# Attention's TensorE work grouped by two units, and one rounding of k moved from ScalarE to GpSimd

## The chip, the cores and the metric

The kernel runs on one core of a Trainium2 chip. The metric is the device time of one execution in microseconds (us). The engines are called as the profile calls them: PE (TensorE, matmuls), PEld (its weight loads), DVE (VectorE), ACT (ScalarE), POOL (GpSimd) and SP (SyncE, which issues most DMAs). Each engine works through its own queue of instructions in a fixed order.

## The reference

Causal attention over 2 batches, 12 heads, 448 positions and a head size of 64 is followed by two feed-forward blocks of width 768 with 3072 hidden units; ahead of the second stands a Fourier mixing. Everything is asked for in 32-bit floats.

```python
scores = q @ k.T / 8 ; scores above the diagonal = -1e9
attn = softmax(scores) ; x = attn @ v                  # heads side by side: x is [2, 448, 768]
x = x + relu(layernorm(x) * g @ w_ch1) @ w_ch2          # first feed-forward
u = x + real(fft(fft(x, over positions), over features))
out = u + relu(layernorm(u) @ w_ch1') @ w_ch2'          # second feed-forward
```

## The kernel before

**Precision.** A product that must be exact to more than one rounded operand is done as three matmuls: each operand is split into a rounded part ("hi", type fp32r) and what is left ("lo"), and hi x lo, lo x hi and hi x hi are added up in PSUM. q is split in `split_q` (POOL for all but the first two pairs), k in `split_k`: the rounded part (scaled by -1/8) is made at L251 by DVE for the first pair and at L253 by ACT for the other eleven; the rest is made by DVE at L254, which reads the rounded part.

**Attention.** The 24 heads are taken as 12 pairs of heads, and each pair as four units (`UNITS`). Units 0 and 1 are query blocks 0 and 2 of either head, unit 2 is query block 1 of both, unit 3 the last 64 queries of both. There are 48 units in all. A unit goes through these steps, each a small function:

- `scores` (PE, L282): the matmuls into PSUM tiles `sps`. Units 0 and 1 are done in one call. The matmuls of units 0 to 2 use 64 rows of the array (the two heads lie in its two halves), those of unit 3 all 128.
- `row_max` (DVE, L299) and `exps` (ACT, L311): mask and row maximum, then exponential and row sum into the SBUF tile `pexp`.
- `transposes` (PE, L355): four 128x128 transposes into a PSUM tile `tps`; `transposed` (ACT, L360) copies it to SBUF as `pT`.
- `values` (PE, L374): the product with v, added up in `avps`. The matmuls use 64 columns of the array for either head. Unit 0 is done with unit 1.

Once a pair: `sum_recip` (DVE, L320 to L323) makes reciprocals of the row sums; `spread` (PE, L330) transposes them and ACT copies them out (`divrow`, L334); `spread_rows` (PE, L340 and L344) spreads them over the partitions and ACT copies the result out (`inv`, L349); `scaled` (DVE, L399) multiplies. For half of the pairs `moved` (POOL, L410 and L411) issues two DMAs that shift the rows by one partition.

**The order.** One loop with step i, one step a unit, writes the whole attention down. In step i of the kernel before, PE gets the transposes of unit i-1, the scores of unit i+3 and the values of unit i-3; DVE gets the row maximum of unit i; ACT gets the copy of unit i-1's transposes and then the exponentials of unit i. Between them lie the splits of q and k for later pairs (`splits`: for pair p at steps 4(p-2) and 4(p-2)+1, the first pairs by `SPLIT_AT`), the loads of the raw q, k and v, and from step 32 on the first loads and conversions of feed-forward weights (`w_load`, `w_tick`: two ACT and four DVE instructions on 128x768 for each weight tile, L167 to L174, L91 and L92). `sum_recip`, `spread` and `spread_rows` come one, two and three steps after the first of the next pair begins. The layer norm of batch 0 (`ln_rest`) is put into the later steps by `bg_step`.

The framework takes this text as priorities: a planner places instructions in each engine's queue by its own estimate of when they can start, so that work of later steps can come ahead of work that it holds to be late. After that the queues are fixed. PSUM tiles `sps`, `tps` and the one of `spread` come from a pool of seven banks, and `avps` has the eighth. A tile takes a bank when the last reader of an earlier one is done.

After attention the feed-forward of batch 0 starts (`ff_lead`, matmuls `hps`), then the rest; nothing there is touched by the change.

Of the kernel before, what the change touches and what calls it, by code (L numbers as in the profile page):

```python
# [14 lines left out]
ACTF = mybir.ActivationFunctionType  # L15
# [4 lines left out]
B, H, S, D = 2, 12, 448, 64  # L20
# [4 lines left out]
PAIRS = [3, 4, 5, 0, 1, 2]  # L25
# [5 lines left out]
ES = 4  # L31
W_LOAD, W_FROM, W_EARLY = 32, 38, 6
SPLIT_AT = {1: (1, 1), 2: (2, 5)}
AHEAD, L_T, L_C, L_V = (3, 1, 2, 3)
Q_AT, K_AT = (0, 1)
NB1, NB2 = 3, 6
NJ = DM // P
HJ = NJ // 2
# [14 lines left out]
def fused_kernel(ctx: ExitStack, tc: tile.TileContext, aps, out):  # L53
    nc = tc.nc
# [147 lines left out]
    q_raw, v_raw, qparts, zparts, kparts = {}, {}, {}, {}, {}  # L202
# [44 lines left out]
    def split_k(b, pr):  # L247
        k = kparts[b, pr] = t_tile([P, 2, S], "ks")
        src = q_raw[b, pr][:, 1]
        if (b, pr) == pairs[0]:  # L250
            yield nc.vector.tensor_scalar_mul(k[:, 0], src, -(D**-0.5))  # L251
        else:
            yield nc.scalar.activation(out=k[:, 0], in_=src, func=ACTF.Copy, scale=-(D**-0.5))  # L253
        yield nc.vector.scalar_tensor_tensor(  # L254
            out=k[:, 1], in0=src, scalar=-(D**-0.5), in1=f32(k[:, 0]), op0=ALU.mult, op1=ALU.subtract
        )
# [5 lines left out]
    def scores(i):  # L262

        b, pr, unit = units[i]
        if i in s_ps:
            return
        q, k, z = qparts[b, pr], kparts[b, pr], zparts[b, pr]
        now = [i, i + 1] if unit == UNITS[0] else [i]
        banks = {}
        for u in now:  # L270
            s_ps[u] = {n: bank("sps") for n in sorted({seg[2] for seg in units[u][2]})}
        work = sorted([(seg[1], u, seg) for u in now for seg in units[u][2]], key=lambda w: w[0])
        for blk in dict.fromkeys(w[0] for w in work):
            segs = [w for w in work if w[0] == blk]
            for qu, ku in ((0, 0), (1, 0), (0, 1)):
                for _, u, (r, blk, at, c, _) in segs:
                    n = min(P * (blk + 1), S)
                    if r is None:
                        lhsT, rhs = z[:, qu], k[:, ku, :n]
                    else:  # L280
                        lhsT, rhs = q[own[r], qu, blk * P : (blk + 1) * P], k[own[r], ku, :n]
                    nc.tensor.matmul(  # L282
                        out=s_ps[u][at][:, c : c + n], lhsT=lhsT, rhs=rhs, start=(qu + ku == 0), stop=(ku == 1),
                        skip_group_check=True,
                    )
# [19 lines left out]
    def exps(i):  # L305
        b, pr, unit = units[i]
        e = exp_tiles[i % ES]
        flat = e.rearrange("p a b -> p (a b)")
        sp, st = s_ps.pop(i), stat[b, pr]
        for col, at, c, to, n in widths(unit):  # L310
            nc.scalar.activation(  # L311
                out=flat[:, to : to + n], in_=sp[at][:, c : c + n], func=ACTF.Exp, scale=-1.0, bias=st[:, 0, col : col + 1],
                accum_out=st[:, 1, col : col + 1],
            )
        p_sb[i] = e

    def sum_recip(b, pr):

        st, d = stat.pop((b, pr)), psm.tile([P, 2, NT], F32R, tag="dv", name="div")
        nc.vector.tensor_scalar_add(st[:, 1], st[:, 1], 1e-9)  # L320
        nc.vector.reciprocal(out=st[:, 2], in_=st[:, 1])
        nc.vector.tensor_copy(out=d[:, 0], in_=st[:, 2])
        nc.vector.tensor_tensor(out=d[:, 1], in0=st[:, 2], in1=f32(d[:, 0]), op=ALU.subtract)  # L323
        diag[b, pr] = d
# [26 lines left out]
    def transposes(i):  # L351
        e = p_sb.pop(i)
        tp = bank("tps")
        for a in range(4):
            nc.tensor.transpose(out=tp[:, a * P : (a + 1) * P], in_=e[:, a], identity=ident)  # L355
        t_ps[i] = tp

    def transposed(i):
        t = t_tile([P, 4, P], "pT", F32)
        nc.scalar.activation(  # L360
            out=t.rearrange("p a q -> p (a q)"), in_=t_ps.pop(i), func=ACTF.Copy
        )
        pT[i] = t

    def values(i):
        b, pr, unit = units[i]
        if unit == UNITS[0]:
            return
        if unit == UNITS[1]:
            av[b, pr] = one_bank("avps")  # L370
        o, vv = av[b, pr], v_raw[b, pr]

        def add(r, cols, key, blocks, p):
            nc.tensor.matmul(  # L374
                out=o[own[r], cols], lhsT=vv[:, r, key], rhs=p, start=(key == 0), stop=(key == blocks - 1),
                skip_group_check=True,
            )

        if unit == UNITS[1]:
            p = pT.pop(i - 1), pT.pop(i)  # L380
            for blk, c in ((0, 0), (2, 1)):
                for key in range(blk + 1):
                    for r in range(2):
                        add(r, slice(blk * P, (blk + 1) * P), key, blk + 1, p[r][:, c + key])
        elif unit == UNITS[2]:
            p = pT.pop(i)
            for key in range(2):
                for r in range(2):
                    add(r, slice(P, 2 * P), key, 2, p[:, 2 * r + key])
        else:  # L390
            p = pT.pop(i)
            for key in range(4):
                for r in range(2):
                    add(r, slice(3 * P, S), key, 4, p[:, key, own[r]])
            del v_raw[b, pr]

    def scaled(b, pr):
        xt = px.tile([P, S], F32, tag="x", name="x") if pr < HJ else p_tile("xr")
        nc.vector.tensor_tensor(out=xt, in0=av.pop((b, pr))[:, :S], in1=inv.pop((b, pr)), op=ALU.mult)  # L399
        xa[b, pr] = xt  # L400
        if pr < HJ:
            x[b, pr] = xt

    def moved(b, pr):

        for j in range(HJ, NJ):
            if (b, j) not in x:
                x[b, j] = px.tile([P, S], F32, tag="x", name="x")
        xt = xa[b, pr]
        nc.gpsimd.dma_start(out=x[b, pr][1:], in_=xt[: P - 1])  # L410
        nc.gpsimd.dma_start(out=x[b, HJ + (pr + 1) % HJ][:1], in_=xt[P - 1 :])  # L411
# [4 lines left out]
    def ln_sum(b, j, src=x):  # L416
        if b not in ln_acc:
            ln_acc[b], n_acc[b] = src[b, j], 1
            return
        acc = ln_acc[b]  # L420
        if n_acc[b] == 1:
            ln_acc[b] = p_tile("lnacc")
        n_acc[b] += 1
        nc.vector.tensor_tensor(out=ln_acc[b], in0=acc, in1=src[b, j], op=ALU.add)
# [270 lines left out]
    def ln_first():  # L695
        now, *after = ln_rest(0, g_sb)
        bg.extend(now)
        late.append(after)

    later = {}  # L700
    i = 0
    while i < n + L_V or max(later, default=0) >= i:
        pi, at = divmod(i, per)
        if 0 <= i - L_T < n:
            transposes(i - L_T)
        while scored <= min(i + AHEAD, n - 1) and units[scored][:2] in kparts:
            scores(scored)
            scored += 1
        if i < n:
            red = row_max(i)  # L710
        if 0 <= i - L_C < n:
            transposed(i - L_C)
        for f in later.pop(i, []):
            f()
        if i == 0:
            exps(0)
        for f, p in splits.pop(i, []):
            for _ in f(*pairs[p]) or ():
                pass
        if at == 2 and pi + 3 < len(pairs):  # L720
            load_pair(*pairs[pi + 3])
        if i >= W_LOAD and n_raw[0] < n_split[0] + 2:
            w_load()
        if i >= W_FROM:
            w_tick(1, W_EARLY)
        with tc.issue_after(red.ins):
            bg_step()
        if 0 < i < n:
            exps(i)
        if 0 <= i - L_V < n:  # L730
            values(i - L_V)
            b, pr, _ = units[i - L_V]
            if (i - L_V) % per == per - 1:
                scaled(b, pr)
                ln_sum(b, pr, xa)
                if pr >= HJ:
                    later.setdefault(i + 1, []).append(lambda b=b, pr=pr: moved(b, pr))
                if (b, pr) == (0, PAIRS[-1]):
                    later.setdefault(i + 1, []).append(lambda: ln_first())
        if i < n and i % per == per - 1:  # L740
            b, pr, _ = units[i]
            later.setdefault(i + 1, []).append(lambda b=b, pr=pr: sum_recip(b, pr))
            later.setdefault(i + 2, []).append(lambda b=b, pr=pr: spread(b, pr))
            later.setdefault(i + 3, []).append(lambda b=b, pr=pr: spread_rows(b, pr))
        i += 1
    raw_ahead[0] = 2
    while bg:
# [145 lines left out]
```

## Time and profile before

| | us |
|---|---|
| median of 3 runs | 860.5 (857.07 to 861.02) |
| the profiled execution | 857.58 |
| its span, first to last instruction | 855.7 |
| attention's first matmul | 4.89 |
| first feed-forward matmul | 107.13 |

| engine | busy us | share of the span |
|---|---|---|
| PE | 841.3 | 98% |
| PEld | 756.6 | 88% |
| DVE | 599.1 | 70% |
| ACT | 331.9 | 39% |
| POOL | 46.0 | 5% |

In a timeline a line gives the start of a group of like instructions in us, how long they took together, the engine, the line of the code, the operation, what it writes and reads, its shape and the count; in brackets stands how long the engine had been idle before and on what. The shape before a matmul's output is rows*columns of the array that it uses. The end of a matmul is modelled, so a matmul's row overlaps the next one's; the distance from start to start is what counts.

### The profile page before, as it was taken

Reading aid. Unit: us, or ns where it says so; the run is one execution under the profiler, and the core shown is the slowest. Engines: PE = TensorE matmul, PEld = TensorE weight load, DVE = VectorE, ACT = ScalarE, POOL = GpSimd, SP = SyncE. Lnnn points to the kernel's source line nnn. Section 1 sums busy time; section 2 is a strip of 40 time slices with the busy share of each in tenths; the row PEclk is TensorE's granted clock in tenths of the full one; section 3 lists DMA queues with packets and bytes.
Section 4 is the critical chain, followed back from the end, with each engine's and each line's share of the span. In section 5 each row is a group of like instructions: output and inputs, shape, how many; then the busy total and the mean of one; then the engine's idle time right before and its main releaser. Section 6 shows DMA issues by size and latency. Waiting matters only on the chain.

```text
span 855.7 us, 11863 instructions
## 1 busy us (share of the span) xinstructions
PE 841.3 (98%) x4664; PEld 756.6 (88%) x4664; DVE 599.1 (70%) x1019; ACT 331.9 (39%) x627; POOL 46.0 (5%) x91
## 2 busy tenths in 40 slices
PE   6999999999999999999999999999999999999997
PEld 5776789899999999999998889899999999999997
DVE  5789999796666566666699789696666566666432
ACT  6898975323332333223234245322332233223200
POOL 5433000100000000000101000000000000000000
PEclk9999999999999999999999999999999999999999
DMA  5434644333333333333615203324333332320011
GB/s 205 136 103 133 201 151 171 117 105 117 111 111 110 111 111 111 111 111 107 204 60 197 74 1 105 117 74 149 110 101 109 102 100 107 111 74 1 1 65 64
DMA packets 21431, 93.28 MB, mean 109 GB/s; under 512 B 2768, under 2 KB 4568, under 8 KB 21376
## 3 DMA queue, kind: packets, MB, share of 16 engines
q1 hardware_dynamic: 19152, 86.68, 29.9%
q0 software_dynamic: 2080, 5.62, 2.1%
q8 instruction: 36, 0.59, 0.3%
q10 hardware_dynamic: 144, 0.23, 0.1%
q14 instruction: 19, 0.16, 0.1%
HBM read 88.40 MB, written 2.75 MB: 107 GB/s over the span
## 4 chain that ended last, share of the span: by engine, by line
PE 93%; DVE 3%; ACT 2%; DMA 1%; issue 1%; DVEq 0%; ACTq 0%; SPq 0%
PE hps L97 14%; PE hps L96 14%; PE hps L95 14%; PE yps L95 14%; PE yps L97 14%; PE yps L96 14%; PE sps L282 2%; PE tps L355 2%; PE avps L374 2%; ACT pexp L311 1%; DVE sps L299 1%; PE mixps L95 1%; PE mixps L96 1%; PE mixps L97 1%; PE abps L95 1%
## 5 line engine op out<-in xcount | busy, mean ns | idle before, releaser
L95 PE MATMUL yps<-h,wsp 128*128 128x448 f32 x576 | 211.3, 367 | 0.0
L97 PE MATMUL hps<-xn,wsp 128*128 128x448 f32 x576 | 211.0, 366 | 0.0
L95 PE MATMUL hps<-xn,wsp 128*128 128x448 f32 x576 | 211.0, 366 | 0.0
L96 PE MATMUL yps<-h,wsp 128*128 128x448 f32 x576 | 210.7, 366 | 0.0
L96 PE MATMUL hps<-xn,wsp 128*128 128x448 f32 x576 | 210.6, 366 | 0.0
L97 PE MATMUL yps<-h,wsp 128*128 128x448 f32 x576 | 210.5, 365 | 0.0
L91 ACT ACTIVATE wsp<-wbits 128x768 fp32r<-128x768 f32 x96 | 80.9, 842 | 171.1 <-PE yps L97 159.2
L167 ACT ACTIVATE wbits<-wraw 128x768 f32<-128x768 f32 x96 | 86.3, 899 | 95.2 <-DVE wsp L92 94.5
L95 PEld LDWEIGHTS hps<-xn,wsp 128*128 128x128 f32 x576 | 108.2, 188 | 9.2 <-issue 0.4
L96 PEld LDWEIGHTS yps<-h,wsp 128*128 128x128 f32 x576 | 108.2, 188 | 9.1 <-issue 0.6
L97 PEld LDWEIGHTS hps<-xn,wsp 128*128 128x128 f32 x576 | 108.2, 188 | 9.1 <-issue 0.2
L96 PEld LDWEIGHTS hps<-xn,wsp 128*128 128x128 f32 x576 | 108.2, 188 | 9.0 <-issue 0.2
L95 PEld LDWEIGHTS yps<-h,wsp 128*128 128x128 f32 x576 | 108.2, 188 | 8.9 <-issue 0.4
L97 PEld LDWEIGHTS yps<-h,wsp 128*128 128x128 f32 x576 | 108.2, 188 | 8.8 <-issue 0.2
L517 ACT ACTIVATE h<-hps 128x448 fp32r<-128x448 f32 x96 | 52.2, 545 | 147.9 <-PE hps L97 147.7
L518 DVE SCALAR_TENSOR_TENSOR h<-hps,h 128x448 fp32r<-128x448 f32 x96 | 59.4, 621 | 69.3 <-ACT h L517 69.2
L539 DVE TENSOR_TENSOR x<-x,yps 128x448 f32<-128x448 f32 x96 | 58.9, 617 | 68.3 <-PE yps L97 68.2
L92 DVE TENSOR_TENSOR wsp<-wbits,wsp 128x768 fp32r<-128x768 f32 x96 | 91.9, 957 | 19.0 <-ACT wsp L91 14.2
L168 DVE TENSOR_SCALAR wbits<-wbits 128x768 uint32<-128x768 uint32 x96 | 53.5, 557 | 64.0 <-ACT wbits L167 63.4
L170 DVE SCALAR_TENSOR_TENSOR wbits<-wraw,wbits 128x768 uint32<-128x768 uint32 x96 | 91.8, 956 | 2.3
L174 DVE SCALAR_TENSOR_TENSOR wbits<-wraw,wbits 128x768 uint32<-128x768 uint32 x96 | 92.0, 959 | 0.4
L311 ACT ACTIVATE pexp<-sps,stat 128x128 f32<-128x128 f32 (+3 forms) x84 | 41.3, 506 | 8.3 <-DVE stat L299 7.6
(123 smaller groups left out, 644.8 us busy)
## 6 DMA issues: line engine op xcount, KB each, us to landing
wraw<-in_w SPq DMA_DIRECT2D x96, 768.0 KB, 4.2
qkv<-in_qk SPq DMA_DIRECT2D x11, 448.0 KB, 4.8
qkv<-in_v SPq DMA_DIRECT2D x12, 256.0 KB, 5.3
out_t<-x SPq DMA_DIRECT2D x12, 224.0 KB, 1.9
x<-xr POOLq DMA_DIRECT2D x6, 222.2 KB, 4.0
cd<-in_cd POOLq DMA_DIRECT2D x3, 386.0 KB, 4.0
sd<-in_sd POOLq DMA_DIRECT2D x3, 386.0 KB, 6.2
cs<-in_cs POOLq DMA_DIRECT2D x2, 448.0 KB, 5.0
```

The lines of the kernel that those rows point to most:

```text
L91: nc.scalar.activation(out=hi, in_=src, func=ACTF.Copy)
L92: nc.vector.tensor_tensor(out=lo, in0=src, in1=f32(hi), op=ALU.subtract)
L95: nc.tensor.matmul(out=dst, lhsT=w_lo, rhs=x_hi, start=first, stop=False)
L96: nc.tensor.matmul(out=dst, lhsT=w_hi, rhs=x_lo, start=False, stop=False)
L97: nc.tensor.matmul(out=dst, lhsT=w_hi, rhs=x_hi, start=False, stop=last)
L167: nc.scalar.activation(out=f, in_=high.bitcast(F32), func=ACTF.Copy, scale=EXPONENTS)
L168: nc.vector.tensor_scalar(out=bits, in0=bits, scalar1=3, scalar2=None, op0=ALU.logical_shift_left)
L170: nc.vector.scalar_tensor_tensor(out=bits, in0=high, scalar=0x80000000, in1=bits, op0=ALU.bitwise_and, op1=ALU.bitwise_or)
L174: nc.vector.scalar_tensor_tensor(out=bits, in0=low, scalar=29, in1=bits, op0=ALU.logical_shift_right, op1=ALU.bitwise_or)
L517: nc.scalar.activation(out=t[:, 0], in_=src, func=ACTF.Relu)
L518: nc.vector.scalar_tensor_tensor(out=t[:, 1], in0=src, scalar=0.0, in1=f32(t[:, 0]), op0=ALU.max, op1=ALU.subtract)
L539: nc.vector.tensor_tensor(out=xx, in0=xx, in1=y, op=ALU.add)
```

## The change

There are two edits. In `split_k` the rounded part of k is made by POOL instead of ACT for the eleven pairs after the first. In attention's loop PE gets its work in even steps alone, for two units at once. The even step i holds, in this order: the transposes of units i-2 and i-1; in the third step of a pair the `spread` of the pair before; the scores of units i+2 and i+3; in the third step of a pair `spread_rows`; further down, behind the row maximum and the exponentials of unit i, the values of units i-4 and i-3. ACT's copy of the transposes comes two steps after the unit instead of one. The exponentials of even units come ahead of the splits instead of behind them. Scores of four units instead of three are written ahead of the loop, and the loop ends one step later.

```diff
-AHEAD, L_T, L_C, L_V = (3, 1, 2, 3)
+AHEAD = 4
...
-            yield nc.scalar.activation(out=k[:, 0], in_=src, func=ACTF.Copy, scale=-(D**-0.5))
+            yield nc.gpsimd.tensor_scalar_mul(k[:, 0], src, -(D**-0.5))
...
-    while i < n + L_V or max(later, default=0) >= i:
+    while i < n + 4 or max(later, default=0) >= i:
         pi, at = divmod(i, per)
-        if 0 <= i - L_T < n:
-            transposes(i - L_T)
-        while scored <= min(i + AHEAD, n - 1) and units[scored][:2] in kparts:
-            scores(scored)
-            scored += 1
+        done = pairs[pi - 1] if 0 < pi <= len(pairs) else None
+        if i % 2 == 0:
+            for u in (i - 2, i - 1):
+                if 0 <= u < n:
+                    transposes(u)
+            if at == 2 and done:
+                spread(*done)
+            while scored <= min(i + 3, n - 1) and units[scored][:2] in kparts:
+                scores(scored)
+                scored += 1
+            if at == 2 and done:
+                spread_rows(*done)
         if i < n:
             red = row_max(i)
-        if 0 <= i - L_C < n:
-            transposed(i - L_C)
+        if i % 2 == 0 and i < n:
+            exps(i)
+        if 0 <= i - 2 < n:
+            transposed(i - 2)
...
-        if i == 0:
-            exps(0)
...
-        if 0 < i < n:
+        if i % 2 and i < n:
             exps(i)
-        if 0 <= i - L_V < n:
-            values(i - L_V)
-            b, pr, _ = units[i - L_V]
-            if (i - L_V) % per == per - 1:
-                scaled(b, pr)
...
+        if at == 0 and done:
+            sum_recip(*done)
+        if i % 2 == 0:
+            for u in (i - 4, i - 3):
+                if 0 <= u < n:
+                    values(u)
+        if at == 2 and done:
+            b, pr = done
+            scaled(b, pr)
...
-        if i < n and i % per == per - 1:
-            b, pr, _ = units[i]
-            later.setdefault(i + 1, []).append(lambda b=b, pr=pr: sum_recip(b, pr))
-            later.setdefault(i + 2, []).append(lambda b=b, pr=pr: spread(b, pr))
-            later.setdefault(i + 3, []).append(lambda b=b, pr=pr: spread_rows(b, pr))
```

## Rows read from the trace of the kernel before

**Rows 1.** The page's first part: busy us, share of the span, instructions.
```profile
PE 841.3 (98%) x4664; PEld 756.6 (88%) x4664; DVE 599.1 (70%) x1019; ACT 331.9 (39%) x627; POOL 46.0 (5%) x91
```

**Rows 2.** Busy time by stretch: its length, engines with counts, granted clock, DMA.
```profile
22.03:60.36 38.33, 38.33 (x420) 29.43 (x416) 30.00 (x114) 33.08 (x108) 16.58 (x29) 1.00 0.36 114
...
69.05:78.72 9.67, 7.93 (x87) 5.96 (x84) 8.36 (x27) 8.49 (x25) 5.29 (x8) 0.99 0.53 180
78.72:95.95 17.23, 16.80 (x168) 12.91 (x166) 17.20 (x56) 16.42 (x47) 2.70 (x6) 0.91 0.53 165
95.95:107.13 11.18, 9.91 (x125) 7.77 (x121) 11.14 (x29) 10.37 (x28) 0.00 (x0) 1.00 0.68 225
107.13:855.70 748.57, 744.27 (x3672) 682.95 (x3672) 514.40 (x739) 241.35 (x359) 10.65 (x15) 1.00 0.30 102
```

**Rows 3.** PE's timeline, one pair of the regular stretch, 50.03 to 57.69.
```profile
50.03 0.28 PE L330 MATMUL invps<-ident,div 128*14 128x128 f32 x1
50.24 0.66 PE L374 MATMUL avps<-pT,qkv 128*64 128x128 f32 x8
50.83 0.66 PE L355 MATMUL tps<-ident,pexp 128*128 128x128 f32 x4
51.42 0.54 PE L340 MATMUL invps<-divrow,pick 14*128 14x128 f32 x3
...
52.09 0.69 PE L374 MATMUL avps<-pT,qkv 128*64 128x64 f32 x16
52.70 0.66 PE L355 MATMUL tps<-ident,pexp 128*128 128x128 f32 x4
53.29 0.62 PE L282 MATMUL sps<-ks,qs 64*128 64x256 f32 x6
53.84 0.66 PE L355 MATMUL tps<-ident,pexp 128*128 128x128 f32 x4
54.25 0.85 PE L282 MATMUL sps<-ks,zd 128*128 128x448 f32 x3
55.03 1.09 PE L374 MATMUL avps<-pT,qkv 128*64 128x128 f32 x16
56.05 0.66 PE L355 MATMUL tps<-ident,pexp 128*128 128x128 f32 x4
56.64 1.12 PE L282 MATMUL sps<-ks,qs 64*128 64x128 f32 x12
57.69 0.28 PE L330 MATMUL invps<-ident,div 128*14 128x128 f32 x1
```

**Rows 4.** PE's timeline at attention's end.
```profile
104.28 2.05 PE L374 MATMUL avps<-pT,qkv 128*64 128x128 f32 x40
```

**Rows 5.** The timeline of the first pairs, ACT, PE and DVE.
```profile
10.45 0.57 ACT L253 ACTIVATE ks<-qkv 128x448 fp32r<-128x448 f32 x1
...
10.91 0.36 ACT L311 ACTIVATE pexp<-sps,stat 128x128 f32<-128x128 f32 x1
...
11.42 0.33 PE L355 MATMUL tps<-ident,pexp 128*128 128x128 f32 x1 [0.73 <-ACT pexp L311]
...
19.45 1.16 DVE L254 SCALAR_TENSOR_TENSOR ks<-qkv,ks 128x448 fp32r<-128x448 f32 x2 [1.25 <-ACT ks L253]
```

**Rows 6.** The timeline around PE's longest wait, ACT and PE.
```profile
76.25 0.91 ACT L167 ACTIVATE wbits<-wraw 128x768 f32<-128x768 f32 x1
...
77.33 0.55 PE L340 MATMUL invps<-divrow,pick 14*128 14x128 f32 x3 [1.71 <-ACT divrow L334]
```

**Rows 7.** Groups by form, 22.03 to 60.36: count, busy us, mean ns, idle before.
```profile
L322 DVE CAST div<-stat 128x7 fp32r<-128x7 f32 x6 | 1.0, 171 | 0.2
...
L241 POOL CAST qs<-qkv 128x448 fp32r<-128x448 f32 x5 | 2.8, 558 | 0.6 <-DMA qkv<-in_qk 0.3
```

**Rows 8.** The timeline of POOL and DVE at one moment.
```profile
76.26 1.14 POOL L242 TENSOR_TENSOR qs<-qkv,qs 128x448 fp32r<-128x448 f32 x1
...
76.47 0.95 DVE L322 CAST div<-stat 128x7 fp32r<-128x7 f32 x1
```

More of the change, by code (lines that the diff above doesn't have):

```diff
@@ L727, in fused_kernel @@
             bg_step()
-        if 0 < i < n:
+        if i % 2 and i < n:
             exps(i)
-        if 0 <= i - L_V < n:
-            values(i - L_V)
-            b, pr, _ = units[i - L_V]
-            if (i - L_V) % per == per - 1:
-                scaled(b, pr)
[L735 to L739, printed above, removed]
-        if i < n and i % per == per - 1:
-            b, pr, _ = units[i]
-            later.setdefault(i + 1, []).append(lambda b=b, pr=pr: sum_recip(b, pr))
-            later.setdefault(i + 2, []).append(lambda b=b, pr=pr: spread(b, pr))
-            later.setdefault(i + 3, []).append(lambda b=b, pr=pr: spread_rows(b, pr))
+        if at == 0 and done:
[7 more added lines that the diff above has]
+            scaled(b, pr)
+            ln_sum(b, pr, xa)
+            if pr >= HJ:
+                later.setdefault(i + 1, []).append(lambda b=b, pr=pr: moved(b, pr))
+            if (b, pr) == (0, PAIRS[-1]):
+                later.setdefault(i + 1, []).append(lambda: ln_first())
         i += 1
```

## The prediction

> **What bounds the kernel now.** I read the page's first part first: PE is busy for 98% of the span and the next engine, DVE, for 70% [rows 1]. So time can be won only where PE's queue gets shorter, or where PE waits. The table of busy time by stretch says where that may be [rows 2]. From 107.13 to the end PE is busy for 744.27 of 748.57 us, and the change touches none of this. What it touches ends at 107.13. There, between 22.03 and 60.36, PE is busy without a break, DVE for 30.00 and ACT for 33.08 of 38.33 us. From 69.05 on PE has idle time: 1.74, 0.43 and 1.27 us in three stretches, and in one of them a granted clock of 0.91.
>
> Then I read PE's timeline of one regular pair [rows 3]. It lasts from 50.03 to 57.69, 7.66 us, and five such pairs fill the stretch (5 x 7.66 = 38.3). The reader is to look at the distance from one group's start to the next one's, and at the array shape before the output. Four transposes followed by matmuls of another shape take 0.59 us (52.70 to 53.29); four followed by matmuls of the same shape 128*128 take 0.41 (53.84 to 54.25). The same shows in the values: the groups of 16, 8 and 16 take 1.02, 0.59 and 0.61 one by one, 2.22 together, while at attention's end 40 in one run take 2.05, of which the last matmul's tail of some 0.08 (52.09 + 0.69 against 52.70) lies beside the next group: 1.97 [rows 4]. So a border between shapes costs 0.18 us after transposes and (2.22 - 1.97) / 2 = 0.12 after values. A pair has eleven groups now, counting the transposes at 53.84 and the scores at 54.25, which share a shape, as one. PE waits for nobody in them; the borders are part of what bounds it.
>
> **The change, part by part.**
>
> *Grouping on PE.* The same matmuls are issued, in another order. In a pair's first step: eight transposes 0.41 + 0.59 = 1.00, scores of unit 2 0.55, of unit 3 0.78, values of units 0 and 1 1.02: 3.35. In its third step: eight transposes 1.00, the spread's transpose 0.21, scores of the next units 0 and 1 1.05, the spreading matmuls 0.67, values of units 2 and 3 0.59 + 0.61 - 0.12 = 1.08: 4.01. The sum is 7.36 against 7.66, 0.30 less a pair. Two groups fewer a pair, nine for eleven, since unit 3's scores lose their neighbour of the same shape.
>
> Whether PE gets this depends on the others. ACT has 33.08 / 5 = 6.62 us a pair, and 6.06 without k; DVE has 6.00 [rows 2]. Half of ACT's is 3.03, which has to fit under PE's 3.35 and 4.01: in two steps it makes two units' exponentials and two copies, and PE takes up both units' transposes at the next even step. The margins are 0.3 and 1.0 us, and the exponentials of the even unit can run earlier, since its scores are a whole even step old. I take the full 0.30 for the five regular pairs: 1.5 us. For the six pairs after them I take it too, 1.8 us, because what is done there on DVE and ACT beside attention (weights, batch 0's norm) is placed by the planner into gaps and is not due before the feed-forward starts. If that cover is gone, the 1.8 is gone.
>
> *PSUM.* In a pair's third step the scores of units 2 and 3 hold three banks, two transposed units two, the spread one and the next two units' scores two: eight from a pool of seven. So the last of these scores have to wait until the exponentials of unit 2 have read its first bank. These scores were written 3.35 us earlier; a unit's share of DVE's and ACT's pair, a quarter of 6.00 and of 6.06, is 1.5 us each, by estimate 3.0 together, so I cost this at nothing. If it waits, the matmuls of the two heads no longer run abreast, which doubles the scores' 1.05 at most: 1.05 a pair.
>
> *k on POOL.* Eleven ACT instructions of some 0.56 us go [rows 5] and eleven POOL ones come. The trace has no such form on POOL; its one-input cast of the same 128x448 takes 0.56 [rows 7], its two-input operation 1.14 [rows 8]. I take 0.56, as it has one input. POOL is busy for 16.58 / 5 = 3.3 us a pair, and nothing of the pair waits on k for several steps, except for pairs 1 and 2. DVE's L254 stands in order behind it: whatever row maximum is queued behind L254 waits too.
>
> *The start.* Up to 22.03 PE waits on others: at 11.42 it had been idle for 0.73 on exponentials, and ACT started those at 10.91, after k's rounded part at 10.45 [rows 5]. With k on POOL they come 0.46 earlier; with 0.30 from the first pair's groups the gain is 0.8. At best DVE's wait of 1.25 for k at 19.45 also goes, 1.5 in all; at worst POOL is a whole instruction late in the first pairs, a loss of 0.6.
>
> *The late stalls.* PE's idle time after 69.05 is 1.74 + 0.43 + 1.27 = 3.4, and the clock of 0.91 over 17.23 us means 1.5 more; 5.0 in all. The longest wait, 1.71, is for ACT's `divrow`, which stood behind weight conversions [rows 6]: an order fixed by the planner. In the new order the spreading matmuls come 0.21 + 1.05 = 1.26 after the spread, now 0.21 + 0.59 + 0.59 = 1.39, so the same accident can happen. ACT loses k twice between 69.05 and 95.95, where it is busy for 24.9 of 26.9 us; I take these 2 x 0.56 = 1.1 us as won. The ends are 5.0 won and, with an accident more like the one at 77.33 and its clock, 3.2 lost.
>
> *Sum.* 1.5 + 1.8 + 0.8 + 1.1 = 5.2 us less. The profiled execution took 857.58, of which 855.7 is span; it would come to 852.4. It lies 2.9 below the median of the runs, 860.5, so for the median I forecast 855.3.
>
> *A rule against it.* At 76.47 a DVE cast of 7 columns took 0.95 us, where such casts take 0.17 on average, and it ended at 77.42, as POOL's instruction of 76.26 did at 77.40 [rows 7, 8]. The Trainium skill, page "SBUF — State Buffer", section "Who interferes with whom", says that GpSimd and VectorE share a pair of ports which one of them locks for a whole instruction, when VectorE's is in a two-port mode or has two SBUF inputs; the trace agrees. By that rule each new POOL instruction could hold DVE for up to 0.56, 6.2 us in all; the regular pairs have 1.66 us of idle DVE each to cover it, but the two in the full stretch would not be covered, and the sum would be 5.2 - 1.1 = 4.1, a median of 856.4.
>
> **The rivals.**
>
> *All stalls go.* If with less on ACT the late waits and the fall of the clock vanish, the gain is 0.8 + 3.3 + 5.0 = 9.1: 851.4. For it speaks that the longest wait is on ACT; against it that DVE is busy for 17.20 of 17.23 us there.
>
> *PE waits at each even step, or the late pairs give it back.* Two units' transposes need the odd unit's exponentials at once. If PE waits for them 0.15 us at each of the 24 even steps, or the bank holds it for 0.3 a pair, the grouping is worth nothing; likewise if the planner, which at the start already cut one unit's transposes in two around scores, cuts the groups of eight. That is also the case in which the change doesn't do what it says. What is left is the start: 860.5 - 0.8 = 859.7. The thin margin of 0.3 speaks for it, the unbroken regular stretch against it.
>
> *DVE waits for POOL.* L254 stands in DVE's queue and POOL's has q's split ahead of k: 0.56 + 1.14 + 0.56 = 2.26 us. Where the planner holds POOL for faster than it is, DVE stands for all of that in each pair, with the row maxima behind it. DVE's pair becomes 6.00 + 2.26 = 8.26 us against 7.66 now, 0.6 x 10 = 6.0 more: 860.5 + 6.0 - 0.8 = 865.7. It decides from a wait of 1.66 us a pair on. Against it: k is split several steps ahead of its use, and in the regular stretch DVE never waited for ACT's k.
>
> **How the numbers follow.** The forecast, 855.3, gets 0.45, all stalls gone 0.14, no net effect 0.28, DVE behind POOL 0.13. About 0.5% (4.3 us) is what a measurement of this kernel can tell from no change, so faster means below 856.2 and slower above 864.8. The forecast's own range, from the late stalls' and the start's bounds, is 852 to 859; three quarters of it I count below 856.2, with the first rival 0.48. The no-effect case and the rest of the forecast make 0.38; the last rival, with its upper half and a stall more, 0.14. The range for 8 in 10 goes from 850.0, past the case without stalls, to 862.5, which leaves out the last rival.
>
> **What would show it.** In PE's timeline between 25 and 60 the transposes stand in groups of eight, the pair's period is 7.36 and PE is idle for nothing: then grouping was right. A period above 7.6 or transposes cut in two say that it was wrong. Waits of L254 on POOL of over 1 us say that the third rival holds. First feed-forward matmul near 102: the sum holds; if it is there and the total hasn't fallen, something behind 107.13 took it back, which I hold for unlikely since PE alone sets the end there.

## The result and the profile after

The changed kernel takes 865.74 us (median; 864.70 to 866.30) against 859.25 of the kernel before in the same comparison: a ratio of 1.0082, with a 95% interval of 1.0063 to 1.0102, so some 7.0 us slower. The forecast of 855.3 was wrong, and its range ended at 862.5. The profiled execution took 865.45 us, 863.0 of it span, against 857.58 and 855.7 before.

One thing ahead was told wrongly: the text says that ACT's copy of the transposes moves from one step after its unit to two. The constants in the diff (`L_C` is 2) say that it is two in both kernels. No number of the prediction rests on it.

First part of the page of the changed kernel, which answers to [rows 1]: busy us, share, instructions.

```profile
PE 844.6 (98%) x4664; PEld 761.4 (88%) x4664; DVE 600.3 (70%) x1019; ACT 328.3 (38%) x616; POOL 62.6 (7%) x102
```

POOL's eleven new instructions brought it 16.6 us more, while ACT lost only 3.6. Next the table by stretch of the changed kernel, with the columns of [rows 2]; the stretches begin at like states of the work, with the transposes that open a pair.

```profile
25.03:33.85 8.82, 8.82 (x88) 7.16 (x84) 5.73 (x22) 7.04 (x23) 4.98 (x7) 0.81 0.35 110
33.85:55.78 21.93, 21.93 (x252) 17.83 (x250) 16.84 (x62) 18.15 (x59) 17.50 (x24) 1.00 0.38 121
...
80.42:91.86 11.44, 8.42 (x86) 6.11 (x84) 11.37 (x31) 8.64 (x24) 4.40 (x6) 1.00 0.46 159
91.86:110.29 18.43, 15.53 (x167) 12.20 (x164) 18.16 (x58) 17.08 (x49) 1.11 (x2) 1.00 0.49 158
110.29:863.00 752.71, 748.42 (x3714) 686.09 (x3711) 515.73 (x741) 242.36 (x362) 10.65 (x15) 1.00 0.30 103
```

The reader is to see three things. The regular stretch is as full on PE as before. From 80.42 on DVE is full (11.37 of 11.44 us) and PE is not (8.42). And a granted clock of 0.81 now stands at 25.03 to 33.85, where before there was 1.00. The start of the same piece of work in both traces says where the time went:

| the transposes that open a pair | before | after | later by |
|---|---|---|---|
| first of the listed | 22.03 | 25.03 | 3.0 |
| one pair on | 29.70 | 33.85 | 4.2 |
| four pairs on | 52.70 | 55.78 | 3.1 |
| six pairs on | 69.05 | 72.45 | 3.4 |
| eight pairs on | 87.78 | 91.86 | 4.1 |
| nine pairs on | 95.95 | 101.16 | 5.2 |
| end of the span | 855.7 | 863.0 | 7.3 |

In these two profiles about four of the seven us were lost before 34, the regular pairs won 1.1 back, and the late pairs and attention's end lost the rest. How much of the first 3.0 is the change's own work they do not say: the granted clock was full from 10.19 in one and from 18.15 in the other. x1 and x2 below, whose order up to there is the same, stood at 25.70 and 22.18 at this place, with the clock full from 21.47 and 10.36. PE's idle time from 72.45 to 110.29 is 0.29 + 3.02 + 2.90 = 6.2 us, where it was 3.4 before.

PE's timeline of one regular pair of the changed kernel, with the columns of [rows 3]:

```profile
41.16 1.09 PE L355 MATMUL tps<-ident,pexp 128*128 128x128 f32 x8
42.18 0.63 PE L282 MATMUL sps<-ks,qs 64*128 64x256 f32 x6
42.73 0.87 PE L282 MATMUL sps<-ks,zd 128*128 128x448 f32 x3
43.54 1.09 PE L374 MATMUL avps<-pT,qkv 128*64 128x128 f32 x16
44.56 1.09 PE L355 MATMUL tps<-ident,pexp 128*128 128x128 f32 x8
45.49 0.27 PE L330 MATMUL invps<-ident,div 128*14 128x128 f32 x1
45.69 1.12 PE L282 MATMUL sps<-ks,qs 64*128 64x128 f32 x12
46.75 0.55 PE L340 MATMUL invps<-divrow,pick 14*128 14x128 f32 x3
47.13 0.35 PE L344 MATMUL invps<-divrow,pick 14*128 14x64 f32 x2
47.42 1.12 PE L374 MATMUL avps<-pT,qkv 128*64 128x128 f32 x24
48.47 0.33 PE L355 MATMUL tps<-ident,pexp 128*128 128x128 f32 x1
```

The groups of eight are there, without a wait, and the pair lasts 48.47 - 41.16 = 7.31 us, against 7.66 before and 7.36 forecast. The first feed-forward matmul, forecast near 102, came at 110.29. POOL's instructions by form, up to 100 us (count, busy us, mean ns, idle before):

```profile
L253 POOL TENSOR_SCALAR ks<-qkv 128x448 fp32r<-128x448 f32 x11 | 15.1, 1369 | 2.0 <-DMA qkv<-in_qk 1.9
...
L241 POOL CAST qs<-qkv 128x448 fp32r<-128x448 f32 x10 | 5.5, 555 | 3.5 <-PE invps L344 3.0
```

The multiplication takes 1.33 us (median; 1.37 on average), 2.4 times the cast on which the forecast's 0.56 rested [rows 7]. The timeline of the start, which answers to [rows 5], shows who pays:

```profile
18.99 1.33 POOL L253 TENSOR_SCALAR ks<-qkv 128x448 fp32r<-128x448 f32 x1
...
20.27 0.56 POOL L241 CAST qs<-qkv 128x448 fp32r<-128x448 f32 x1
...
20.35 0.95 DVE L254 SCALAR_TENSOR_TENSOR ks<-qkv,ks 128x448 fp32r<-128x448 f32 x1 [1.60 <-POOL ks L253]
...
21.22 0.42 DVE L299 CUSTOM_DVE_ANT_0 sps<-sps,maskw 128x256 f32<-128x256 f32 x1
...
21.80 0.47 ACT L311 ACTIVATE pexp<-sps,stat 128x256 f32<-128x256 f32 x1 [2.46 <-DVE stat L299]
...
23.00 0.25 ACT L334 ACTIVATE divrow<-invps 14x128 fp32r<-14x128 f32 x1
...
23.30 0.55 PE L340 MATMUL invps<-divrow,pick 14*128 14x128 f32 x3 [1.53 <-ACT divrow L334]
```

It is read from top to bottom. DVE stands 1.60 us at L254 for POOL. The row maximum queued behind it is late, ACT's exponentials wait 2.46 for that, `divrow` stands in ACT's queue behind the exponentials, and PE waits 1.53 for `divrow`. At 24.98 the granted clock then falls to half (1.2 GHz) until 28.39. PE's own timeline shows what that costs, eight transposes in 1.89 us (25.03 to 26.92) instead of 1.02:

```profile
23.98 1.12 PE L374 MATMUL avps<-pT,qkv 128*64 128x128 f32 x24
25.03 1.97 PE L355 MATMUL tps<-ident,pexp 128*128 128x128 f32 x8
26.92 1.01 PE L282 MATMUL sps<-ks,qs 64*128 64x256 f32 x6
```

### The profile page after: what moved, and what is told of

The parts are those of the page before. It is cut to its first block, busy times and chain, and to the rows that moved or that the text cites. A ratio compares the mean times of both kernels' runs of the same rounds, so it can differ in the third digit from the quotient of the medians.

```text
span 863.0 us, 11858 instructions
## 1 busy us (share of the span) xinstructions
PE 844.6 (98%) x4664; PEld 761.4 (88%) x4664; DVE 600.3 (70%) x1019; ACT 328.3 (38%) x616; POOL 62.6 (7%) x102
## 4 chain that ended last, share of the span: by engine, by line
PE 93%; DVE 3%; ACT 2%; POOL 1%; issue 1%; DMA 0%; ACTq 0%; DVEq 0%
PE hps L96 14%; PE hps L97 14%; PE hps L95 14%; PE yps L95 14%; PE yps L97 14%; PE yps L96 14%; PE sps L282 2%; PE tps L355 2%; PE avps L374 2%; ACT pexp L311 1%; DVE sps L299 1%; PE mixps L95 1%; PE mixps L96 1%; PE mixps L97 1%; PE abps L95 1%
```

## The experiments

The kernel before ran again in each comparison (medians 858.01 to 859.67), so ratios are compared and not medians; microseconds that are worked out from ratios go by 859.5. Line numbers shift by a few from one kernel to the next (L254 is L255 in x7 and x9). First the two edits apart, then k made by others, then the grouping cut to stretches, then DVE's order.

**e1, grouping alone.** The changed kernel with k back on ACT.

```diff
-            yield nc.gpsimd.tensor_scalar_mul(k[:, 0], src, -(D**-0.5))
+            yield nc.scalar.activation(out=k[:, 0], in_=src, func=ACTF.Copy, scale=-(D**-0.5))
```

> Grouping alone: k's rounded part goes back to ACT. Theory A (the loss is POOL's 1.33 us instruction and DVE's waits of 6.9 us in all behind it): the grouping's 0.35 us a pair shows, DVE never waits over 0.3 us at L254, first feed-forward matmuls run on from about 104, time 853 to 857 against 859.25 before. Theory B (the grouping itself starves ACT and DVE in the late pairs, whoever makes k): PE still idles for 4 us or more after 69, time 862 to 867.

Measured: 862.23 us, ratio 1.0039 (1.0026 to 1.0052). Grouping alone is slower, by 3.4 us.

**e2, POOL alone.** The kernel before with k on POOL.

```diff
-            yield nc.scalar.activation(out=k[:, 0], in_=src, func=ACTF.Copy, scale=-(D**-0.5))
+            yield nc.gpsimd.tensor_scalar_mul(k[:, 0], src, -(D**-0.5))
```

> The order of before, with k's rounded part on POOL alone. Theory A: DVE waits at L254 for POOL as in the changed kernel, and with no gain of the grouping against it the time is 864 to 870. Theory B: the order of before bears k on POOL, 858 to 861.

Measured: 860.61, ratio 1.0018 (1.0005 to 1.0031), 1.5 us slower. The parts make 3.4 + 1.5 = 4.9, both together 7.0. The 2.1 between them is no more than what the three intervals leave open, so that the two edits hinder each other is not shown here.

**e3, k on DVE,** in the grouped order.

```diff
-            yield nc.gpsimd.tensor_scalar_mul(k[:, 0], src, -(D**-0.5))
+            yield nc.vector.tensor_scalar_mul(k[:, 0], src, -(D**-0.5))
```

> Grouping, with k's rounded part on DVE (the form that took 0.39 us for the first pair), so that L254 waits for no other engine. Theory A: 852 to 857, as good as k on ACT or better, since ACT keeps its 0.56 us a pair. Theory B: 862 to 867.

Measured: 860.64, ratio 1.0034 (1.0021 to 1.0047), by its median between the two expectations. Even with the work added to DVE itself, it is better than waiting for POOL, and no better than ACT.

**e4, a plain cast on POOL,** in the grouped order. The kernel leaves out the factor -1/8 for the eleven pairs, so it computes other values; the queues keep every instruction in its place, and only POOL's eleven have another form.

```diff
-            yield nc.gpsimd.tensor_scalar_mul(k[:, 0], src, -(D**-0.5))
+            yield nc.gpsimd.tensor_copy(out=k[:, 0], in_=src)
+            yield nc.vector.scalar_tensor_tensor(
+                out=k[:, 1], in0=src, scalar=1.0, in1=f32(k[:, 0]), op0=ALU.mult, op1=ALU.subtract
+            )
+            return
```

> Grouping, k's rounded part on POOL by its plain cast (0.56 us) instead of the multiplying form (1.33 us); k's scale by -1/8 is left out for the eleven pairs, nothing else. Theory A: with 0.77 us less an instruction DVE's waits at L254 fall from 6.9 to under 3 us in all, time 854 to 859. Theory B: as the changed kernel, 864 to 867.

Measured: 860.54, ratio 1.0014 (1.0002 to 1.0026), and DVE's waits at L254 fall from 6.9 to 3.5 us. So the length of POOL's instruction is worth 0.0068 x 859.5 = 5.8 us. In e4's trace PE's wait of the start is gone: from 6 to 60 us it waits for nobody, and the clock, full from 18.51, stays so until 86.78. But with the very 0.56 that the forecast took (the median of the eleven), the change still wins nothing. The theory that POOL holds the whole loss missed in all four.

**x1, grouped in the regular stretch alone** (steps 8 to 27), k on ACT. The loop takes either order by step; with the grouped order nowhere, every engine's queue is that of the kernel before.

```diff
+TWO_FROM, TWO_TO = (8, 28)
...
+        two = TWO_FROM <= i < TWO_TO
+        if not two or i % 2 == 0:
+            while n_t < min(i, n):
+                transposes(n_t)
+                n_t += 1
...
```

> PE's work grouped by two units in steps 8 to 27 alone, the order of before ahead of them and behind them; k's rounded part on ACT as before. Theory S (the grouping gains where nothing else is short, and loses in the start and in the late pairs): five pairs gain 0.35 each, 1.7 in all, PE's clock is full from about 10.5 as in the ungrouped orders, and the first feed-forward matmul comes near 105.5: ratio 0.997 to 0.999, 857 to 859. Rival (the gain in the regular stretch is given back behind it in any order, since DVE and ACT set the late pairs): the regular pairs are as short, but the late pairs start earlier and end as before, ratio 1.000 to 1.001, first feed-forward matmul near 107.

Measured: 858.56, ratio 0.9987 (0.9975 to 0.9999). The gain of the regular pairs reaches the end, 1.1 of the 1.7. PE's timeline of x1, just behind the regular stretch, shows a wait of 0.8 into which the rest may have gone (an estimate, 1.7 - 0.8 = 0.9 against the 1.1):

```profile
64.29 0.87 PE L381 MATMUL avps<-pT,qkv 128*64 128x128 f32 x10 [0.80 <-DVE x L406]
```

It is a wait for `scaled`; every grouped kernel has it there, of 0.79 or 0.80 us (at 63.97 in the changed kernel), and the kernel before has not. The expectation of the clock fell: it was full from 21.47 only, though the start is ungrouped.

**x2, grouped from step 8 to the end.**

```diff
-TWO_FROM, TWO_TO = (8, 28)
+TWO_FROM, TWO_TO = (8, 99)
```

> Grouped from step 8 to attention's end, the start in the order of before, k on ACT. Compared with the kernel grouped throughout with k on ACT (ratio 1.0039) it gives the start's share, compared with the one grouped in steps 8 to 27 alone the late pairs' share. Theory S, with the start at 1.6 to 3.0 lost by the clock at half until 18.5: 0.0019 to 0.0035 less, ratio 1.0005 to 1.002. Rival (the late pairs hold the whole loss, an earlier start is only waited off there): ratio 1.003 to 1.004, no gain from the better start.

Measured: 861.43, ratio 1.0023 (1.0010 to 1.0035). It lies between the two expectations. Against e1 the start's share of the loss is 0.0016, 1.4 us, though these two intervals overlap; against x1 the late pairs' share is 0.0036, 3.1 us, and those do not. The forecast had 1.8 the other way there. PE's timeline of x2 shows its longest wait in the late pairs:

```profile
85.35 1.90 PE L289 MATMUL sps<-ks,qs 64*128 64x128 f32 x11 [1.61 <-ACT pexp L318]
```

Behind it the clock is at half from 85.45 to 92.28. In x1 the longest wait there is 1.23, and the clock stays full.

**x4, as x1 with k by a plain cast on POOL;** here the factor -1/8 is taken over by the row maximum.

> As the kernel grouped in steps 8 to 27 alone, and k's rounded part is a plain cast on POOL (0.56 by its trace, the factor -1/8 taken over by the row maximum). Theory S with k's length as the price of POOL: the cast frees ACT of 11 x 0.56 and costs DVE little, so it is as fast as the one with k on ACT or up to 1.0 faster: 856 to 858.5, ratio 0.996 to 0.999. Rival (DVE, which stands in order behind POOL, loses in the late pairs whatever the length): 1.0 to 2.0 slower than the one with k on ACT, ratio 0.999 to 1.001.

Measured: 856.73, ratio 0.9967 (0.9950 to 0.9984): faster than both kernels.

**x5, the subtraction behind.** The changed kernel; from the third pair on DVE's L254 is written one or two steps after POOL's multiplication. PE's and ACT's queues are instruction by instruction those of the changed kernel.

```diff
-            for _ in f(*pairs[p]) or ():
-                pass
+            g = f(*pairs[p])
+            if g and p > 1:
+                next(g)
+                rest.setdefault(i + (1 if p == 2 else 2), []).append(g)
+            elif g:
+                for _ in g:
+                    pass
+        for g in rest.pop(i, []):
+            next(g)
```

(For the third pair it is the multiplication that is written a step earlier, at step 4 instead of 5. With that, two of POOL's multiplications stand ahead of parts of q's split that they followed before.)

> The changed kernel with one thing moved: from the third pair on DVE's subtraction that reads k's rounded part is written one or two steps behind POOL's multiplication, no longer right behind it. POOL's eleven multiplications of 1.3 us stay. Theory W (what POOL's length costs is DVE standing in its queue for it): DVE's waits on POOL's k fall from 6.9 us to under 2.5, what is left is the first split's 1.6, and the time falls by 2 to 4: 861.5 to 863.5, ratio 1.002 to 1.0045. Rival (the length costs by what POOL and DVE hold against each other while both run, or by work that comes late anyway): waits gone, time as in the changed kernel, 865 to 866.5, ratio 1.006 to 1.008.

Measured: 859.52, ratio 0.9999 (0.9987 to 1.0010). That is 0.0083, 7.1 us (6.2 by the medians), from subtractions that stand elsewhere in DVE's queue and two multiplications that stand elsewhere in POOL's, more than expected, and the reason given was half wrong: the waits on POOL didn't fall. DVE's timeline in the changed kernel, two regular pairs:

```profile
38.58 0.70 DVE L254 SCALAR_TENSOR_TENSOR ks<-qkv,ks 128x448 fp32r<-128x448 f32 x1 [1.55 <-POOL ks L253]
...
46.22 0.70 DVE L254 SCALAR_TENSOR_TENSOR ks<-qkv,ks 128x448 fp32r<-128x448 f32 x1 [1.89 <-POOL ks L253]
```

and in x5, from 14 to 28 us:

```profile
16.16 0.95 DVE L254 SCALAR_TENSOR_TENSOR ks<-qkv,ks 128x448 fp32r<-128x448 f32 x1 [0.74 <-POOL ks L253]
...
18.78 1.11 DVE L254 SCALAR_TENSOR_TENSOR ks<-qkv,ks 128x448 fp32r<-128x448 f32 x1
...
26.98 0.70 DVE L254 SCALAR_TENSOR_TENSOR ks<-qkv,ks 128x448 fp32r<-128x448 f32 x1 [2.15 <-POOL ks L253]
```

In sum 6.9 us of waits there and 7.7 here. The long ones of the regular stretch stand in both, right before `sum_recip`, and cost nothing: the pair of 7.31 shown above holds the wait of 46.22. What differs is the start, where 1.60 has become 0.74 and nothing, and the place of the late ones. So more than the "one thing" of the expectation was moved.

**x7, the same for the two pairs split in the start alone.**

```diff
-            if g and p > 1:
+            if g and 1 < p < 4:
```

> The changed kernel with the subtraction moved behind POOL's multiplication for the third and fourth pair alone, the two that are split in the start; the later pairs as in the changed kernel. Theory W-start (the wait of 1.60 at 20.35, with the row maximum behind it, PE's wait and its half clock behind that, is where the 6.2 came from; in the regular stretch PE is never late for such waits): 4 to 6 of the 6.2 come back, 859.7 to 861.7, ratio 1.000 to 1.0025. Rival (the wait of 1.61 at 78.93 in the late pairs holds most): 1 to 2.5 come back, 863 to 864.7, ratio 1.004 to 1.006.

Measured: 861.19, ratio 1.0025 (1.0013 to 1.0036): 0.0057, 4.9 us, come back by the splits of two pairs. POOL and DVE in x7's timeline show what moved:

```profile
14.79 1.33 POOL L253 TENSOR_SCALAR ks<-qkv 128x448 fp32r<-128x448 f32 x1
...
16.15 0.95 DVE L255 SCALAR_TENSOR_TENSOR ks<-qkv,ks 128x448 fp32r<-128x448 f32 x1
...
16.59 1.70 POOL L253 TENSOR_SCALAR ks<-qkv 128x448 fp32r<-128x448 f32 x1
...
19.17 0.71 DVE L255 SCALAR_TENSOR_TENSOR ks<-qkv,ks 128x448 fp32r<-128x448 f32 x1
```

In the changed kernel the multiplications start at 16.70 and 18.99, and the two subtractions stand one right behind the other, at 18.06 and 20.35. In x7 both multiplications come some 2 us earlier, the third pair's subtraction stands earlier as well, and only the fourth pair's stands behind row maxima. Which of these moves holds the 4.9 was not tried. The later pairs are the cleaner case: x5 and x7 differ in DVE's queue alone, by those pairs' subtractions, and there the place is worth 0.0026, 2.2 us, with intervals that do not overlap.

PE's timeline of x7, over the place where the changed kernel waited:

```profile
20.80 1.13 PE L283 MATMUL sps<-ks,qs 64*128 64x128 f32 x12
21.87 0.55 PE L341 MATMUL invps<-divrow,pick 14*128 14x128 f32 x3
...
22.54 1.12 PE L375 MATMUL avps<-pT,qkv 128*64 128x128 f32 x24
23.59 1.09 PE L356 MATMUL tps<-ident,pexp 128*128 128x128 f32 x8
```

From the scores to the spreading matmuls it is 1.07 us, without a wait, where it was 2.65 (20.65 to 23.30), and the clock stays full. Both profiles have their first full clock at nearly the same time, 18.83 and 18.15, so the comparison is fair. The last long wait, 1.41 on `divrow` at 108.41, and the half clock of 110.31 to 113.73 are gone too; x7 has one stretch at half clock, 97.33 to 100.75, for the changed kernel's two. Between the two profiles 2.8 us are there at the first feed-forward matmul (107.46 against 110.29) and 2.2 come behind it, where the changed kernel's second half clock lies.

**x8 and x9, controls:** the subtraction behind with k on ACT, in the order of before (x8) and in the grouped one (x9, which is e1 with x5's edit).

> A control: the kernel before, with k on ACT, and DVE's subtraction written one or two steps behind. Theory W (the moved place gains because it takes POOL's length out of DVE's queue): ACT's rounding is done early here, nothing to gain, ratio 0.999 to 1.001. Rival (the place of the subtraction is worth 2 us or more by itself, POOL or not): 855 to 857.5, ratio 0.994 to 0.9975.

> The same control in the grouped order, k on ACT. Grouped with k on ACT and the subtraction in its old place had ratio 1.0039 and DVE waits on ACT's k of 2.1 us, the longest 0.6. Theory W: up to 1 us is won, ratio 1.0025 to 1.004. Rival (the place itself is worth what it was with POOL, 6.2): ratio 0.997 to 0.999, 857 to 859.

Measured: x8 859.53, ratio 1.0001 (0.9989 to 1.0014); x9 858.65, ratio 0.9993 (0.9978 to 1.0008). In the order of before the place is worth nothing, as expected. In the grouped order it is worth 0.0046, 4.0 us, with ACT as well, which is the rival's direction: my theory, that it counts only because POOL is long, falls. But x9 is no move of DVE's instruction alone: ACT's queue is another too, with the two roundings at 14.53 and 16.67 that e1 has in one run at 18.64. DVE's timeline of e1 in two places of the early pairs, then of x9:

```profile
28.14 1.67 DVE L254 SCALAR_TENSOR_TENSOR ks<-qkv,ks 128x448 fp32r<-128x448 f32 x1 [0.57 <-ACT ks L253]
29.73 0.62 DVE L299 CUSTOM_DVE_ANT_0 sps<-sps,maskf 128x448 f32<-128x448 f32 x1
...
36.04 1.08 DVE L254 SCALAR_TENSOR_TENSOR ks<-qkv,ks 128x448 fp32r<-128x448 f32 x1 [0.35 <-ACT ks L253]
37.05 0.62 DVE L299 CUSTOM_DVE_ANT_0 sps<-sps,maskf 128x448 f32<-128x448 f32 x1
```

```profile
25.08 1.66 DVE L255 SCALAR_TENSOR_TENSOR ks<-qkv,ks 128x448 fp32r<-128x448 f32 x1
27.52 0.35 DVE L321 TENSOR_SCALAR stat<-stat 128x7 f32<-128x7 f32 x1 [0.78 <-ACT pexp L312]
```

In e1 a row maximum of unit 3 (`maskf`) stands right behind the subtraction, and PE's next even step wants the exponentials of both units; in x9 the subtraction stands behind the pair's last row maximum, and only `sum_recip` follows. PE waits 0.64 us on `divrow` at 31.43 in e1, and for nobody from 18 to 59 in x9.

**x6, the two findings together:** x4 with the subtraction behind.

> The kernel grouped in steps 8 to 27 alone with k as a plain cast on POOL (ratio 0.9967), and DVE's subtraction for k written one or two steps behind POOL's cast. Theory W (DVE's waits on POOL that have a row maximum right behind them are the price of POOL): its waits on POOL were 1.6 in all, so at most 1.6 is left to win: 855.2 to 856.7, ratio 0.995 to 0.997. Rival (the place of the subtraction is worth some us by itself, as the step from 865.7 to 859.5 was more than the 2 to 4 expected): 853 to 855, ratio 0.992 to 0.995.

Measured: 855.15, ratio 0.9964 (0.9949 to 0.9979). It is the best of all, though not to be told from x4.

**x11, x12, x10:** the same with the grouped order throughout; with k on ACT; and with nothing grouped.

```diff
-TWO_FROM, TWO_TO = (8, 28)
+TWO_FROM, TWO_TO = (0, 99)     # x11; (8, 28) with k on ACT is x12; (99, 99) is x10
```

(x11 also writes scores of four units ahead of the loop, as the changed kernel does.)

> Grouped throughout, k a plain cast on POOL (0.56), DVE's subtraction one or two steps behind it. With k on ACT the same kernel had ratio 0.9993, with POOL's multiplication of 1.33 it had 0.9999, with the cast and the subtraction in its old place 1.0014. Theory L (with DVE's queue in order the late pairs no longer lose by grouping, and ACT gains the eleven roundings): ratio 0.995 to 0.997, as the kernel grouped in steps 8 to 27 alone. Rival (the late pairs still give 2 to 3 back, since PE finds the exponentials late there): 0.9985 to 1.0.

Measured: 858.02, ratio 0.9987 (0.9974 to 1.0000), 2.0 us above x6 by the middle values, with intervals that overlap a little. That is where the rival puts it. The start is grouped here too, so the 2.0 is not the late pairs' alone. The table by stretch of x11, from the first late pair to the last transposes:

```profile
62.94:105.05 42.11, 37.29 (x394) 28.75 (x393) 40.78 (x120) 38.41 (x107) 7.82 (x14) 1.00 0.46 159
```

DVE is busy for 40.78 of 42.11 us, PE for 37.29. Fewer borders on PE can't shorten that. x6, with the old order there, is as full on DVE (33.43 of 34.70 us, 64.40 to 99.10).

> Grouped in steps 8 to 27 alone, k on ACT, the subtraction one or two steps behind. Without the last it had ratio 0.9987; with the cast on POOL and the last it had 0.9964. Theory (the five regular pairs give 1.7 and little stands in the way, so the cast on POOL is worth the rest, 1 to 2 us): ratio 0.997 to 0.9985. Rival (the place of the subtraction brings the difference, the cast nothing): 0.9955 to 0.9968.

Measured: 857.93, ratio 0.9996 (0.9980 to 1.0011). That is above both expectations, and no gain of the place over x1 (0.9987). Against x6 the cast on POOL is worth 0.0032, 2.7 us by the middle values, above the 1 to 2 expected; the two intervals just miss each other.

> The order of before, k a plain cast on POOL, the subtraction one or two steps behind. Nothing is grouped. With k on ACT this order and place had ratio 1.0001, with POOL's multiplication in the old place 1.0018. Theory (ACT is not late in the order of before, so freeing it wins nothing, and a cast of 0.56 costs nothing): 0.999 to 1.001. Rival (ACT's eleven roundings are what the late stalls wait for, and half of the predicted 5.2 comes without grouping): 0.9965 to 0.998.

Measured: 863.87, ratio 1.0061 (1.0038 to 1.0084), which neither expected. Its regular pairs take 8.09 us (39.92 to 48.01) instead of 7.66. The timeline of one, ACT, DVE and PE:

```profile
40.86 0.58 ACT L319 ACTIVATE pexp<-sps,stat 128x384 f32<-128x384 f32 x1
...
41.41 0.55 ACT L357 ACTIVATE inv<-invps 128x448 f32<-128x448 f32 x1
...
42.00 0.62 DVE L407 TENSOR_TENSOR xr<-avps,inv 128x448 f32<-128x448 f32 x1 [1.05 <-ACT inv L357]
...
42.68 1.09 PE L382 MATMUL avps<-pT,qkv 128*64 128x128 f32 x16 [0.21 <-DVE xr L407]
```

ACT copies `inv` behind exponentials, DVE's `scaled` waits 1.05 for it, and PE's values wait for the one bank of `avps`, in this pair and the next two. With k gone from ACT, the planner had arranged ACT's and DVE's queues anew. That shows this wait; five pairs 0.43 longer would make 2.2 of the 5 us against x8, so more than this is in it. It also says that e1 and e2, whose queues the planner arranged anew as well, hold more than the one instruction that their edits name.

## Why the prediction was wrong, by its own steps

- **Grouping, regular pairs (5 x 0.30).** Right: 0.35 a pair, and x1 shows that 1.1 of it reaches the end.
- **Grouping, late pairs (6 x 0.30 = 1.8 less).** Wrong in sign: 3.1 us more (x2 against x1); x11 against x6, where the start is grouped too, has 2.0. The step said that DVE's and ACT's other work there is placed into gaps. There were no gaps: [rows 2] had DVE at 17.20 of 17.23 and 11.14 of 11.18 us, rows that I used against a rival and not against this term.
- **PSUM (nothing).** Right for the regular pairs: the twelve scores at 45.69 take 1.06 without a wait. In a late pair PE stood 1.83 us for a bank, more than the bound of 1.05 and in the pair's first step, not its third: the scores waited for ACT's `inv`, which stood in its queue behind a weight conversion, and that waited for DVE, which had stood 1.61 for POOL. It is the accident of [rows 6] with another copy of ACT's. x5, where DVE's wait is 1.01, still has PE's 1.8, so POOL is not its whole cause. The timeline of the changed kernel there:

```profile
78.93 0.96 DVE L254 SCALAR_TENSOR_TENSOR ks<-qkv,ks 128x448 fp32r<-128x448 f32 x1 [1.61 <-POOL ks L253]
...
82.93 0.84 ACT L91 ACTIVATE wsp<-wbits 128x768 fp32r<-128x768 f32 x1 [1.67 <-DVE wbits L174]
...
83.68 0.53 ACT L349 ACTIVATE inv<-invps 128x448 f32<-128x448 f32 x1
...
84.35 0.85 PE L282 MATMUL sps<-ks,zd 128*128 128x448 f32 x3 [1.83 <-ACT inv L349]
```

- **k on POOL (0.56, harmless).** This step failed most. The size was 1.33, above the two-input operation's 1.14 too, and e4, which changes this size alone, puts its cost at 5.8 of the 12.2 us between the forecast's 5.2 less and the 7.0 more. And the sentence "whatever row maximum is queued behind L254 waits too" had no price in the sum. The price is not the wait but what stands behind it: 1.89 us cost nothing in a regular pair; the start's two splits hold 4.9 us with all that follows (x7).
- **The start (0.8 less).** Wrong: PE waits 1.53 where it did not, and a half clock follows. With clocks that became full at like times the changed kernel opens the pair at 25.03, x8 in the old order at 24.41 and x7 at 23.59. That is 0.6 lost, the worst case named there, and 0.8 won once the splits are out of the way. What had no term was the half clock behind the wait, in which the pair of 25.03 takes 8.82 us instead of 7.31.
- **The late stalls (1.1 less).** Wrong: PE's idle time there grew from 3.4 to 6.2 us.
- **The rival "DVE waits for POOL"** gave 865.7, and 865.74 was measured, but by another sum. It had 0.6 us in each of ten pairs; the regular pairs pay nothing, the start pays most, and the late pairs lose by grouping as well. The hit on the number is chance; the engine and the line were right. Its chance of 0.13 was low, because the argument against it, no waits of DVE on k in the regular stretch, was read in the one stretch where it doesn't matter.
- **The rule on shared ports.** In the timeline of the start DVE's L254 takes 0.95 us beside POOL's cast of 20.27 to 20.83, where its shortest is 0.62. The Trainium skill (page "SBUF — State Buffer", section "Who interferes with whom") says that a VectorE instruction with two SBUF inputs contends with a GpSimd one that reads SBUF. The trace agrees in direction, with 0.33 us more over an overlap of 0.48. It was no large part here: all of DVE's work took 600.3 us, 1.2 more than before. x5 and x9 (0.9999 and 0.9993) say less, since x9 keeps on ACT the work that x5 takes from it.

What stays open: why grouping is sensitive to DVE's order where the old order is not (x8 against x9) was read from rows, not tried alone; which of the moves at the start holds x7's 4.9; and in how far the later start of the clock, below, belongs to the change.

## What to carry to other kernels

Price an instruction that is moved to another engine by a row of the same operation, not of one like it, and look at what stands in order behind its reader: the same wait is worth nothing in one place and, with all that follows it, up to five us in another. A gain on the engine that bounds one stretch counts only in stretches that it bounds; read the busy row of each before multiplying. When an order of work gets coarser, look again at each small instruction ahead of the ones that it now needs in pairs.

## What the runs showed of the hardware

POOL's multiplication of 128x448 by a constant takes 1.33 us, its cast of the same tile 0.56.

The moment of the first full clock differs between profiles: 9.9 to 10.8 us in six of the kernels (the one before among them), 18.2 to 21.5 in eleven. Neither the grouping nor POOL decides it: x8 gives PE the first pairs in the order of the kernel before, but for the place of two small matmuls, and was at 18.68 where that was at 10.19, and x9, grouped, was at 9.91. x8 stood 2.4 us later in the same work for it (24.41 against 22.03). x1 and x2 are the plainest pair: with the same order on every engine over the first pairs, one was at 21.47 and the other at 10.36, and x1 stood 3.5 us later. So of the 3.0 us at 25.03 in the first table a good part may be this, and the comparisons above go by ratios of many runs. What decides it stays open.
